# Attention, a gated layer and a mixture of experts on one core: operands of the second layer made at steps of a table, and the last 24 steps of the first layer written by hand

## The chip, the cores and the metric

The kernel runs on one core of a Trainium2 chip. The metric is the device time of one execution in microseconds. TensorE (PE) multiplies, VectorE (DVE), ScalarE (ACT) and GpSimd (POOL) prepare operands and empty the accumulators in PSUM, and the SyncE queue (SP) issues all the transfers. Each engine works through its own instruction list strictly in order; instructions of different engines wait for each other through semaphores.

## The reference

Cut to what is computed:

```python
a   = softmax(p k^T / 8) v                 # 4 batches x 8 heads, 32 packed rows
o   = softmax(q a^T / 8) a                 # 576 rows of each head
x   = o as [2304, 512]
h   = x @ w_in                             # first layer, 512 -> 2048
x   = (h * sigmoid(1.702 h)) @ w_out       # 2048 -> 512
pr  = domain_probs / sum(domain_probs)
out = sum over 4 experts e of pr[:, e] * (relu(x @ w1[e]) @ w2[e])   # second layer, 512 -> 1024 -> 512
```

All inputs are 32 bit floats or wider, and the kernel keeps that precision on TensorE by splitting each operand into a high part (a cast on ACT) and a low part (source minus high part, a subtraction on POOL or DVE), with three matmuls (high·high, low·high, high·low) for each product.

## The kernel before

**First layer.** The tokens are cut into 8 blocks of 288, the hidden width into 4 passes of 512. In a step of a pass `l1_first(a, j, c)` makes hidden chunk c of block j (6 matmuls of 288 columns into one PSUM bank; then two gelu activations on ACT, one giving the high part, and a DVE subtraction on L547 giving the low part), and `l2_first` multiplies the hidden values of the block before with `w_out` (12 matmuls, L556; DVE adds the result to `y` on L581). Step (j, c) below is `l2_first` of block j, chunk of rows c; beside it stands `l1_first` of block j+1. The low part of the last hidden chunk of block j is wanted by the end of step (j, 0).

**Second layer.** 2304 tokens are three pairs of 2 x 384; for each pair 16 quads follow (4 experts x 4 chunks of 256 hidden units), 48 in all, numbered from 0. In a quad, `quad(n)` makes the hidden values by a seven-product scheme (Winograd's form of Strassen's): step k = 0 to 6 holds product k, 6 matmuls of 384 columns on L702, with adds on DVE (L728 to L742), relu on ACT (L710) and the low part on DVE (L711). In steps 1 to 6 `l2_second(n-1, t)` follows, one 128-token tile of the quad before times `w2` (6 matmuls of 512 columns, L765), and DVE adds it, scaled by the probability, to `o` (L776; on ACT, L774, for a pair's first quad). Step 7 has no matmul.

**Operands of the second layer.** The weights of quad n+1 are made during quad n by `w1_operand`: sums s1 to s4 on DVE (L671 to L675), then four casts and subtractions (ACT L156, POOL L157) for S2 and S3; A11 and A12; A22; S1 and S4. Product 0 uses A11, product 1 S2, product 2 S3, product 3 S1, product 4 A12, product 5 A22, product 6 S4. `w2_operand(n)` makes the two halves of `w2` of quad n, which are wanted in quad n+1. The tokens of a pair need four differences T1, T2, T4, T3 (`t_sums`, POOL L618) and for each of seven names a cast of two parts (ACT L636) and two subtractions, one on DVE and one on POOL (L637): `b_operand`, called B0 to B6 below, one for each product. Quads 15 and 31 are the last of a pair (switch quads): during them the next pair's B operands are made, and the T differences in quads 14 and 30.

**What sets the order.** Up to the last 4 steps of the first layer a scheduler of the framework places instructions after its own estimate of times; from there on (L931) each engine gets its instructions in the order in which the code writes them. All operands are generators: each `next` runs one part, at the step where it stands (L949 to L958 for the second layer, `beside` on L922 to L927 for the first pair's). 29 slots of 4.6 KB a partition hold weights, sums and operands; a transfer into a slot waits until the slot's last readers are done. The transfers stand in SP's queue in the order written; during the first quad of a pair the finished rows of the pair before are stored from `l2_second` (L781), and the loads `fetch_w2(n + 1)` at step 5 and `fetch_w1(n + 2)` at the start of the next quad stand behind them.

Of the kernel before, what the change touches and what calls it, by code (L numbers as in the profile page):

```python
# [102 lines left out]
def packed_attention_moe_kernel(  # L103
# [13 lines left out]
    nc = tc.nc  # L117
    B, H, S, D = q.shape
# [11 lines left out]
    CPP = 4  # L130
# [3 lines left out]
    NPAIR = NT // (2 * TB)  # L134
# [14 lines left out]
    def slot(shape, dt, name):  # L149
        return big.tile(shape, dt, tag="b", name=name)  # L150
# [4 lines left out]
    def split(hi, lo, src, eng):  # L155
        nc.scalar.copy(out=hi, in_=src)  # L156
        eng.tensor_sub(out=lo, in0=src, in1=hi.bitcast(F32))  # L157
# [10 lines left out]
    quads = [(i, e, c) for i in range(NPAIR) for e in range(NE) for c in range(w1.shape[2] // 256)]  # L168
    raws = {}
    W = {}  # L170
# [29 lines left out]
    def make_w():  # L200
        order.drain(convert())
# [450 lines left out]
    def w1_operand(n):  # L652


        raw = raws.pop(("w1", n))
        Am = {f"A{m + 1}{k + 1}": raw[:, 2 * k:2 * k + 2, m * 128:(m + 1) * 128] for m in range(2) for k in range(2)}
        S = slot([128, 4, 2, 128], F32, "s")
        s2, s3, s1, s4 = (S[:, x] for x in range(4))

        def operand(names, src):  # L660
            t = slot([128, 2, 2, 2, 128], F32R, "w1")
            hi, lo = t[:, :, 0], t[:, :, 1]
            if len(names) == 1:
                hi, lo = t[:, 0, 0], t[:, 0, 1]
            split(hi, lo, src, nc.gpsimd)
            for o, name in enumerate(names):
                for hl in range(2):
                    for kk in range(2):
                        Wop[n, name, hl, kk] = t[:, o, hl, kk, :]

        nc.vector.tensor_add(out=s1, in0=Am["A21"], in1=Am["A22"])  # L671
        nc.vector.tensor_sub(out=s2, in0=s1, in1=Am["A11"])
        yield
        nc.vector.tensor_sub(out=s3, in0=Am["A11"], in1=Am["A21"])  # L674
        nc.vector.tensor_sub(out=s4, in0=Am["A12"], in1=s2)  # L675
        yield
        operand(("S2", "S3"), S[:, 0:2])
        yield
        yield
        operand(("A11", "A12"), raw[:, :, :128].rearrange("p (o k) f -> p o k f", k=2))  # L680
        yield
        operand(("A22",), Am["A22"])
        yield
        operand(("S1", "S4"), S[:, 2:4])
        yield

    def w2_operand(n):
        raw = raws.pop(("w2", n))
        for c in range(2):
            yield  # L690
            w = W2[n, c] = slot([128, 2, 512], F32R, "w2")
            split(w[:, 0, :], w[:, 1, :], raw[:, c, :], nc.gpsimd)
            yield

    def product(n, k):
        i = quads[n][0]
# [100 lines left out]
    moe = [(packed_w, (0, 0), None)]  # L797
# [22 lines left out]
    pos = {"m": 0}  # L820
# [16 lines left out]
    def moe_step():  # L837
        fn, args, tag = moe[pos["m"]]
        pos["m"] += 1
        part = fn(*args)  # L840
        if part is not None:
            order.drain(part)
        due["n"] = max(due["n"], todo.get(tag, 0))
        if state["cvt"] < due["n"]:
            make_w()
        for part in beside.get(tag, ()):
            next(part, None)
# [10 lines left out]
    def load(what):  # L858
        for t in what.split():
            if t == "F":  # L860
                fetch_w()
            elif (t[0], int(t[1])) not in loaded:
                loaded.add((t[0], int(t[1])))
                (load_kv if t[0] == "k" else load_q)(int(t[1]))
# [4 lines left out]
    def lane(steps):  # L869

        steps = steps.split()
        for i, t in enumerate(steps):
            u = int(t[1])
            need = "kq"[t[0] == "u"] + t[1]
            load(need)
            yield lambda: when[need[0], u]
            part = pack(u) if t[0] == "p" else unpack(u)
            ask = next(part)
            for n in range(1 << 30):
                if n == AHEAD and i + 1 < len(steps):  # L880
                    load("kq"[steps[i + 1][0] == "u"] + steps[i + 1][1])
                t_ = yield ask
                order.at["now"] = t_
                try:
                    ask = part.send(t_)
                except StopIteration:
                    break
            if t[0] == "u":
                finished.append(u)
# [15 lines left out]
    with tc.manual_schedule(engines=engines):  # L905
# [4 lines left out]
        lanes = [lane(x) for x in LANES] + [conversions(2 * CPP, MORE)]  # L910
        for x, back in zip(lanes + [moe_lane()], BACK):
            order.add(x, back)
# [3 lines left out]
    t_parts = {i: t_sums(i) for i in range(NPAIR)}  # L916
    b_parts = {i: b_operand(i) for i in range(NPAIR)}
    last = n_pass1 - 1
    fetch_w1(0)
    fetch_w2(0)  # L920
    first = w1_operand(0)
    beside = {}  # L922
    for c in range(CPP):
        beside["first", last, 3, c] = (t_parts[0],)
        beside["first", last, 4, c] = (first,)
        beside["first", last, 5, c] = (b_parts[0], first)
        beside["first", last, 6, c] = (b_parts[0],)  # L927
    while pos["m"] < len(moe) - CPP:
        moe_step()
    per_pair = len(quads) // NPAIR  # L930
    with tc.manual_schedule(engines=engines):  # L931

        for n in range(len(quads) + 1):
            none = iter(())
            now = quad(n) if n < len(quads) else none
            fetch_w1(n + 1)
            (load_probs, norm_probs)[n]() if n < 2 else None
            after = w1_operand(n + 1) if n + 1 < len(quads) else none
            w2_now = w2_operand(n) if n < len(quads) else none
            tiles = list(range(2 * TB // 128))  # L940
            for k in range(8):
                next(now, None)
                if k > 0:
                    if n == 0:
                        if pos["m"] < len(moe):
                            moe_step()
                    elif tiles:
                        l2_second(n - 1, tiles.pop(0))
                next(after, None)  # L949
                next(w2_now, None)  # L950
                if k == 5:
                    fetch_w2(n + 1)
                after_pair = n // per_pair + 1
                if after_pair < NPAIR:
                    if n % per_pair == per_pair - 2:
                        next(t_parts[after_pair], None)
                    if n % per_pair == per_pair - 1 and k > 0:
                        next(b_parts[after_pair], None)  # L958


# [28 lines left out]
```

## Time and profile before

| | |
|---|---|
| median of 3 runs | 1195.77 us (1195.07 to 1196.13) |
| the profiled execution | 1195.29 us |
| its span, first to last instruction | 1193.5 us |
| mean granted TensorE clock | 0.986 |
| PE busy | 1153.0 us, 97% |
| DVE, ACT, POOL busy | 902.9, 512.0, 465.2 us |

The profile is of one execution. The span lies inside the measured time, 1.8 us short of it. A row of the timeline gives the start in us from the span's start, the length, the engine, the line, the tiles written and read, the shape and how many instructions were merged; in brackets stands how long the engine was idle before, and what it waited for. A row of the waits gives the total, the number of times and the longest one.

### The profile page before, as it was taken

To read this page: it belongs to the slowest core of one execution; us is meant where nothing else is said; L and a number is where in the kernel's file an instruction comes from. 1 tells how busy PE (TensorE), PEld (TensorE's weight loads), DVE (VectorE), ACT (ScalarE), POOL (GpSimd) and SP (SyncE) were. 2 spreads that over 40 slices of the span, in tenths; PEclk is the share of its full clock that TensorE was granted. 3 is DMA by queue.
4 is the path that set the end of the run, shared out by engine and by line. 5 is a ranking of instruction groups with operands and counts; after the bars stand their busy time and mean duration, and the time that the engine had idled before them with its cause. 6 is when DMAs were issued, how large, how long until landed. Compare 5 with 4: busy or idle time off the path is not lost.

```text
span 1193.5 us, 18705 instructions
## 1 busy us (share of the span) xinstructions
PE 1153.0 (97%) x7040; PEld 1045.8 (88%) x7040; DVE 902.9 (76%) x1673; ACT 512.0 (43%) x1144; POOL 465.2 (39%) x385
## 2 busy tenths in 40 slices
PE   6689999999999999999999999999999999999998
PEld 5467899999999898988989878988888788898887
DVE  4976987868766767777778967777779687777775
ACT  4677764444344443333333443333334443333331
POOL 2231211101102434444446754444448554444441
PEclk7799999999999999999999999999999999999999
DMA  9732211211100122222221142222111322211211
GB/s 260 208 118 80 88 54 54 71 53 55 37 18 1 20 71 71 71 71 71 71 70 37 54 141 71 71 71 71 62 45 54 127 86 71 71 57 54 67 54 53
DMA packets 66026, 87.49 MB, mean 73 GB/s; under 512 B 7312, under 2 KB 47248, under 8 KB 65936
## 3 DMA queue, kind: packets, MB, share of 16 engines
q1 hardware_dynamic: 65936, 86.30, 23.9%
q8 instruction: 55, 0.90, 0.3%
q14 instruction: 35, 0.29, 0.1%
HBM read 81.56 MB, written 4.72 MB: 72 GB/s over the span
## 4 chain that ended last, share of the span: by engine, by line
PE 80%; DVE 11%; ACT 3%; DMA 2%; issue 2%; POOL 1%; SPq 0%; DVEq 0%; POOLq 0%; ACTq 0%
PE ps_o L765 29%; PE ps_p L702 25%; PE ps_acc L556 15%; PE ps_h L527 7%; PE ps_w L495 1%; DVE o L776 1%; ACT h L710 1%; DVE h L711 1%; DVE b L637 1%; PE ps_s L311 1%; PE ps_t L298 1%; DVE pw L513 1%; POOL w L157 1%; DMA raw<-in_moe_w_dram 1%; DMA kv<-in_v_dram 1%
## 5 line engine op out<-in xcount | busy, mean ns | idle before, releaser
L765 PE MATMUL ps_o<-w,h 128*128 128x512 f32 x1728 | 445.5, 393 | 0.0
L702 PE MATMUL ps_p<-b,w 128*128 128x384 f32 x2016 | 399.3, 336 | 7.2 <-ACT w L156 3.7
L702 PEld LDWEIGHTS ps_p<-b,w 128*128 128x128 f32 x2016 | 357.9, 188 | 36.8 <-POOL w L157 5.8
L765 PEld LDWEIGHTS ps_o<-w,h 128*128 128x128 f32 x1728 | 320.0, 188 | 50.4
L157 POOL TENSOR_TENSOR w<-raw,w 128x512 fp32r<-128x512 f32 x192 | 229.7, 1196 | 230.7 <-ACT w L156 202.0
L776 DVE SCALAR_TENSOR_TENSOR o<-ps_o,pr,o 128x512 f32<-128x512 f32 x270 | 201.6, 747 | 47.4 <-PE ps_o L765 47.4
L556 PE MATMUL ps_acc<-h,wout 128*128 128x288 f32 x1536 | 230.8, 298 | 4.4 <-DVE h L547 3.7
L556 PEld LDWEIGHTS ps_acc<-h,wout 128*128 128x128 f32 x1536 | 214.4, 190 | 6.9 <-DVE h L547 4.6
L157 POOL TENSOR_TENSOR w<-s,w 128x512 fp32r<-128x512 f32 x96 | 125.2, 1304 | 163.4 <-ACT w L156 163.4
L527 PE MATMUL ps_h<-a,pw 128*128 128x288 f32 x768 | 124.6, 298 | 0.0
L156 ACT CAST w<-s 128x512 fp32r<-128x512 f32 x96 | 58.8, 613 | 126.9 <-DVE s L674 126.9
L527 PEld LDWEIGHTS ps_h<-a,pw 128*128 128x128 f32 x768 | 110.3, 189 | 1.7 <-issue 0.9
L156 ACT CAST w<-raw 128x512 fp32r<-128x512 f32 x192 | 106.6, 555 | 4.9 <-DMA raw<-in_moe_w_dram 4.9
L547 DVE TENSOR_TENSOR h<-g,h 128x288 fp32r<-128x288 f32 x128 | 67.5, 530 | 52.8 <-ACT g L544 52.1
L543 ACT ACTIVATE h<-ps_h 128x288 fp32r<-128x288 f32 x128 | 53.0, 414 | 117.4 <-PE ps_h L527 116.9
L710 ACT ACTIVATE h<-c 128x384 fp32r<-128x384 f32 x48 | 25.2, 525 | 106.7 <-DVE c L736 106.7
L245 POOL TENSOR_TENSOR wout<-cvt,wout 128x512 fp32r<-128x512 f32 x16 | 20.7, 1295 | 114.5 <-ACT wout L243 110.3
L245 POOL TENSOR_TENSOR win<-cvt,win 128x512 fp32r<-128x512 f32 x16 | 21.1, 1321 | 110.7 <-ACT win L243 103.0
L581 DVE TENSOR_TENSOR y<-ps_acc,y 128x288 f32<-128x288 f32 (+2 forms) x120 | 45.0, 391 | 16.5 <-PE ps_acc L556 16.2
L710 ACT ACTIVATE h<-u 128x384 fp32r<-128x384 f32 x48 | 25.2, 525 | 71.5 <-DVE u L742 71.5
L671 DVE TENSOR_TENSOR s<-raw 128x256 f32<-128x256 f32 x48 | 45.2, 942 | 11.9 <-DMA raw<-in_moe_w_dram 6.5
L710 ACT ACTIVATE h<-uv 128x384 fp32r<-128x384 f32 x48 | 25.2, 525 | 67.0 <-DVE uv L742 67.0
(99 smaller groups left out, 1122.8 us busy)
## 6 DMA issues: line engine op xcount, KB each, us to landing
raw<-in_moe_w_dram SPq DMA_DIRECT2D x96, 512.0 KB, 4.0
raw<-in_moe_w_in_dram SPq DMA_DIRECT2D x16, 512.0 KB, 4.5
raw<-in_moe_w_out_dram SPq DMA_DIRECT2D x16, 512.0 KB, 3.7
kv<-in_k_dram SPq DMA_DIRECT2D x16, 288.0 KB, 8.5
q<-in_q_dram SPq DMA_DIRECT2D x32, 144.0 KB, 3.7
out_dram<-o SPq DMA_DIRECT2D x12, 256.0 KB, 2.0
kv<-in_v_dram SPq DMA_DIRECT2D x16, 144.0 KB, 6.8
kv<-in_v_dram SPq DMA_DIRECT2D x8, 288.0 KB, 6.5
```

The lines of the kernel that those rows point to most:

```text
L156: nc.scalar.copy(out=hi, in_=src)
L157: eng.tensor_sub(out=lo, in0=src, in1=hi.bitcast(F32))
L527: nc.tensor.matmul(out=ps[:, :HS], lhsT=PW[a, b, g][:, wp, c * 128:(c + 1) * 128], rhs=A[b * UG + g][:, xp, s * HS:(s + 1) * HS], start=(m ...
L543: nc.scalar.activation(out=h[:, 0, :], in_=ps[:, :HS], func=AF.Gelu_apprx_sigmoid)
L547: nc.vector.tensor_sub(out=h[:, 1, :], in0=g32, in1=h[:, 0, :].bitcast(F32))
L556: nc.tensor.matmul(out=ps[:, :HS], lhsT=W["out", a, c][:, wp, t * 128:(t + 1) * 128], rhs=hid[a, j, c // 2][:, 2 * (c % 2) + hq, :], start ...
L581: nc.vector.tensor_add(out=dst, in0=src, in1=dst)
L671: nc.vector.tensor_add(out=s1, in0=Am["A21"], in1=Am["A22"])
L702: nc.tensor.matmul(out=ps, lhsT=Wop[n, a, wp, kk], rhs=Bop[i, b, xp, kk], start=(m == 0), stop=(m == 5),)
L710: nc.scalar.activation(out=h[:, 0, :], in_=src, func=AF.Relu)
L765: nc.tensor.matmul(out=ps, lhsT=h[:, c, hq, o:o + 128], rhs=W2[n, c][:, wp, :], start=(c == 0 and m == 0), stop=(c == 1 and m == 2),)
L776: nc.vector.scalar_tensor_tensor(out=acc, in0=ps, scalar=pr[:, tok, e:e + 1], in1=acc, op0=ALU.mult, op1=ALU.add,)
```

## The change

`w1_operand` and `w2_operand` return lists of parts instead of being generators, and each part is placed by a table: `W1_AT` and `W2_AT` say at which of a quad's 8 steps it stands, `W1_SWITCH` and `W2_SWITCH` do so for quads 15, 31 and 47. The T differences stand at steps counted back from the pair's first quad (-20 is quad 13, step 4; -17 quad 13, step 7; -13 and -11 quad 14, steps 3 and 5), the B operands at -7, -7, -6, -4, -3 (quad 15, steps 1, 1, 2, 4, 5) and at 1 and 2 of the pair's first quad. For the first pair `FIRST_PAIR` spreads sums (T, W) and operands (W, B) over the steps (3, 0) to (6, 3) of the first layer's last pass. The last 24 steps before the final 4 (the first is `l1_first` of block 5, chunk 0) move under `manual_schedule`, so that from there on every engine has the written order. TensorE's list and SP's are the same in both kernels, instruction for instruction; only DVE, ACT and POOL change.

```diff
--- before.py
+++ after.py
@@ -28,6 +28,14 @@
 UNITS_DONE = 6
 MORE = 4
 AHEAD = 10
+BY_HAND = 24
+W1_AT = (1, 1, 2, 3, 4, 5)
+W1_SWITCH = (1, 1, 2, 4, 5, 4)
+W2_AT = (0, 4)
+W2_SWITCH = (2, 3)
+T_AT = (-20, -17, -13, -11)
+B_AT = (-7, -7, -6, -4, -3, 1, 2)
+FIRST_PAIR = ("", "", "WT", "TT", "TWWB", "WB", "", "", "BW", "BW", "BW", "B", "", "B", "", "B")
 BACK = (0, -0.29, 0.6, 0.7)
 
 
@@ -668,29 +676,31 @@
                     for kk in range(2):
                         Wop[n, name, hl, kk] = t[:, o, hl, kk, :]
 
-        nc.vector.tensor_add(out=s1, in0=Am["A21"], in1=Am["A22"])
-        nc.vector.tensor_sub(out=s2, in0=s1, in1=Am["A11"])
-        yield
-        nc.vector.tensor_sub(out=s3, in0=Am["A11"], in1=Am["A21"])
-        nc.vector.tensor_sub(out=s4, in0=Am["A12"], in1=s2)
-        yield
-        operand(("S2", "S3"), S[:, 0:2])
-        yield
-        yield
-        operand(("A11", "A12"), raw[:, :, :128].rearrange("p (o k) f -> p o k f", k=2))
-        yield
-        operand(("A22",), Am["A22"])
-        yield
-        operand(("S1", "S4"), S[:, 2:4])
-        yield
+        def sums_a():
+            nc.vector.tensor_add(out=s1, in0=Am["A21"], in1=Am["A22"])
+            nc.vector.tensor_sub(out=s2, in0=s1, in1=Am["A11"])
+
+        def sums_b():
+            nc.vector.tensor_sub(out=s3, in0=Am["A11"], in1=Am["A21"])
+            nc.vector.tensor_sub(out=s4, in0=Am["A12"], in1=s2)
+
+        return [
+            sums_a,
+            sums_b,
+            lambda: operand(("S2", "S3"), S[:, 0:2]),
+            lambda: operand(("A11", "A12"), raw[:, :, :128].rearrange("p (o k) f -> p o k f", k=2)),
+            lambda: operand(("A22",), Am["A22"]),
+            lambda: operand(("S1", "S4"), S[:, 2:4]),
+        ]
 
     def w2_operand(n):
         raw = raws.pop(("w2", n))
-        for c in range(2):
-            yield
+
+        def one(c):
             w = W2[n, c] = slot([128, 2, 512], F32R, "w2")
             split(w[:, 0, :], w[:, 1, :], raw[:, c, :], nc.gpsimd)
-            yield
+
+        return [lambda c=c: one(c) for c in range(2)]
 
     def product(n, k):
         i = quads[n][0]
@@ -918,25 +928,28 @@
     last = n_pass1 - 1
     fetch_w1(0)
     fetch_w2(0)
-    first = w1_operand(0)
+    first = (f() for f in w1_operand(0))
     beside = {}
-    for c in range(CPP):
-        beside["first", last, 3, c] = (t_parts[0],)
-        beside["first", last, 4, c] = (first,)
-        beside["first", last, 5, c] = (b_parts[0], first)
-        beside["first", last, 6, c] = (b_parts[0],)
-    while pos["m"] < len(moe) - CPP:
+    for at, what in enumerate(FIRST_PAIR):
+        beside["first", last, 3 + at // CPP, at % CPP] = [{"T": t_parts[0], "B": b_parts[0], "W": first}[x] for x in what]
+    while pos["m"] < len(moe) - CPP - BY_HAND:
         moe_step()
     per_pair = len(quads) // NPAIR
     with tc.manual_schedule(engines=engines):
-
+        while pos["m"] < len(moe) - CPP:
+            moe_step()
+
+        later = []
         for n in range(len(quads) + 1):
             none = iter(())
             now = quad(n) if n < len(quads) else none
             fetch_w1(n + 1)
             (load_probs, norm_probs)[n]() if n < 2 else None
-            after = w1_operand(n + 1) if n + 1 < len(quads) else none
-            w2_now = w2_operand(n) if n < len(quads) else none
+            switch = n % per_pair == per_pair - 1
+            if n + 1 < len(quads):
+                later += [(8 * n + at, f) for at, f in zip(W1_SWITCH if switch else W1_AT, w1_operand(n + 1))]
+            if n < len(quads):
+                later += [(8 * n + at, f) for at, f in zip(W2_SWITCH if switch else W2_AT, w2_operand(n))]
             tiles = list(range(2 * TB // 128))
             for k in range(8):
                 next(now, None)
@@ -946,16 +959,15 @@
                             moe_step()
                     elif tiles:
                         l2_second(n - 1, tiles.pop(0))
-                next(after, None)
-                next(w2_now, None)
+                for at, part in [x for x in later if x[0] == 8 * n + k]:
+                    part()
                 if k == 5:
                     fetch_w2(n + 1)
-                after_pair = n // per_pair + 1
-                if after_pair < NPAIR:
-                    if n % per_pair == per_pair - 2:
-                        next(t_parts[after_pair], None)
-                    if n % per_pair == per_pair - 1 and k > 0:
-                        next(b_parts[after_pair], None)
+                for i in range(1, NPAIR):
+                    when_ = 8 * (n - i * per_pair) + k
+                    for part, slots in ((t_parts[i], T_AT), (b_parts[i], B_AT)):
+                        for x in range(slots.count(when_)):
+                            next(part, None)
 
 
 # ---- launch: one core; inputs and outputs as the reference has them ----
```

In the listings a `w` of 128x2x256 from `raw` is A11 and A12, one of 128x256 from `raw` is A22, one from `s` is S2 and S3 or S1 and S4, one of 128x512 is half a `w2`; line numbers of the changed kernel are 8 to 10 higher.

ACT in the first layer's last pass, before: L543 and the row behind it are a chunk's gelus, and the first row is S2 and S3 of quad 0.

```order
L156 CAST w_4977<-s 128x2x256
L636 CAST b<-y_1062 128x384 x2
L636 CAST b<-T_4838 128x384
L156 CAST w_5038<-raw_2077 128x2x256
L543 ACTIVATE h<-ps_h 128x288
L544 ACTIVATE g_4848<-ps_h 128x288
L636 CAST b<-T_4838 128x384
L156 CAST w_5072<-raw_2077 128x256
L636 CAST b<-T_4893 128x384 x2
L543 ACTIVATE h<-ps_h 128x288
L544 ACTIVATE g_4875<-ps_h 128x288
L156 CAST w_5107<-s 128x2x256
```

The two gelu pairs, of steps (4, 3) and (5, 0) of `l1_first`, stand among ten casts that the scheduler put there. The same engine and place now, from the gelus of `l1_first` of block 5, chunk 0:

```order
L551 ACTIVATE h<-ps_h 128x288
L552 ACTIVATE g_4906<-ps_h 128x288
L164 CAST w_4928<-s 128x2x256
L644 CAST b<-y_1062 128x384 x2
L551 ACTIVATE h<-ps_h 128x288
L552 ACTIVATE g_4944<-ps_h 128x288
L164 CAST w_4962<-raw_2077 128x2x256
L644 CAST b<-T_4892 128x384 x2
L551 ACTIVATE h<-ps_h 128x288
L552 ACTIVATE g_4978<-ps_h 128x288
L551 ACTIVATE h<-ps_h 128x288
L552 ACTIVATE g_5003<-ps_h 128x288
```

The gelu pairs of block 4 are now all ahead of the first cast, and a step has one weight cast and one pair of B casts at most, or none.

POOL in quads 13 and 14 before: T_7359 is T1, T_7383 T2, T_7405 T4 and T_7430 T3, and the first row is S1 and S4 of quad 14.

```order
L157 TENSOR_TENSOR w_7340<-s,w_7340 128x2x256
L618 TENSOR_TENSOR T_7359<-y_1521 128x768
L157 TENSOR_TENSOR w_7380<-raw_7320,w_7380 128x512
L618 TENSOR_TENSOR T_7383<-y_1521,T_7359 128x768
L157 TENSOR_TENSOR w_7402<-s,w_7402 128x2x256
L618 TENSOR_TENSOR T_7405<-y_1521,T_7383 128x768
L157 TENSOR_TENSOR w_7427<-raw_7320,w_7427 128x512
L618 TENSOR_TENSOR T_7430<-y_1521 128x768
L157 TENSOR_TENSOR w_7450<-raw_7343,w_7450 128x2x256
L157 TENSOR_TENSOR w_7471<-raw_7343,w_7471 128x256
L157 TENSOR_TENSOR w_7494<-s,w_7494 128x2x256
```

All four differences stand in quad 14, between its weight subtractions. POOL at the same place now (T_7302 is T1, T_7345 T2, T_7428 T4, T_7477 T3); the first row is half of `w2` of quad 13.

```order
L165 TENSOR_TENSOR w_7299<-raw_7177,w_7299 128x512
L626 TENSOR_TENSOR T_7302<-y_1521 128x768
L165 TENSOR_TENSOR w_7322<-s,w_7322 128x2x256
L626 TENSOR_TENSOR T_7345<-y_1521,T_7302 128x768
L165 TENSOR_TENSOR w_7361<-raw_7325,w_7361 128x512
L165 TENSOR_TENSOR w_7402<-s,w_7402 128x2x256
L165 TENSOR_TENSOR w_7425<-raw_7347,w_7425 128x2x256
L626 TENSOR_TENSOR T_7428<-y_1521,T_7345 128x768
L165 TENSOR_TENSOR w_7448<-raw_7347,w_7448 128x256
L165 TENSOR_TENSOR w_7451<-raw_7325,w_7451 128x512
L165 TENSOR_TENSOR w_7472<-s,w_7472 128x2x256
L626 TENSOR_TENSOR T_7477<-y_1521 128x768
```

T1 and T2 have moved into quad 13, T4 and T3 stand late in quad 14.

ACT from step 4 of quad 15 into quad 16, before: `h<-p` is the relu behind product 4, and the row after it casts A11 and A12 of quad 16.

```order
L710 ACTIVATE h_7499<-p_7508 128x384
L156 CAST w_7612<-raw_7497 128x2x256
L636 CAST b<-T_7359 128x384 x2
L710 ACTIVATE h_7499<-uv 128x384
L156 CAST w_7639<-raw_7497 128x256
L636 CAST b<-y_1521 128x384 x2
L710 ACTIVATE h_7500<-u 128x384
L156 CAST w_7667<-s 128x2x256
L636 CAST b<-T_7405 128x384 x2
L636 CAST b<-y_1521 128x384 x2
L724 COPY p_7692<-ps_p 128x384
L156 CAST w_7717<-raw_7642 128x512
```

Four pairs of B casts follow that of A11 and A12, two of them after the quad's last relu. The same engine from step 3 of quad 15 now, `h<-c` being the relu behind product 3:

```order
L720 ACTIVATE h_7501<-c_7578 128x384
L164 CAST w_7591<-raw_7475 128x512
L720 ACTIVATE h_7500<-p_7509 128x384
L164 CAST w_7612<-raw_7497 128x2x256
L164 CAST w_7615<-s 128x2x256
L644 CAST b<-T_7302 128x384 x2
L720 ACTIVATE h_7500<-uv 128x384
L164 CAST w_7642<-raw_7497 128x256
L644 CAST b<-y_1521 128x384 x2
L720 ACTIVATE h_7501<-u 128x384
L734 COPY p_7682<-ps_p 128x384
L164 CAST w_7684<-raw_7645 128x512
```

The cast of A11 and A12 still stands behind the relu of product 4 in this quad, S1 and S4 directly behind it, and only two B operands are cast between it and the next quad's first copy (`p<-ps`).

## Rows read from the trace of the kernel before

**Rows 1.** Part 1 of the page: busy us, share of the span, instructions
```profile
PE 1153.0 (97%) x7040; PEld 1045.8 (88%) x7040; DVE 902.9 (76%) x1673; ACT 512.0 (43%) x1144; POOL 465.2 (39%) x385
```
**Rows 2.** Waits, 330 us to the end: total us, times, longest
```profile
PE ps_p L702 <- ACT w L156: 3.7, 4, 1.2
PE ps_p L702 <- POOL w L157: 3.5, 6, 0.8
...
PE ps_acc L556 <- DVE h L547: 2.8, 2, 1.5
```
**Rows 3.** Timeline of PE, steps (3, 1), (4, 0) and (4, 3)
```profile
381.83 1.78 PE L556 MATMUL ps_acc<-h,wout 128*128 128x288 f32 x12
...
389.04 1.22 PE L556 MATMUL ps_acc<-h,wout 128*128 128x288 f32 x8
...
401.05 1.23 PE L556 MATMUL ps_acc<-h,wout 128*128 128x288 f32 x8
```
**Rows 4.** Busy time by stretch: us, PE, PEld, DVE, ACT, POOL, clock, DMA
```profile
394.00:398.00 4.00, 4.00 (x21) 4.00 (x21) 4.00 (x6) 2.46 (x7) 4.00 (x4) 0.57 0.00 0
```
**Rows 5.** Timeline of PE: first products of quads 16, 17, 19, 20, 32, 35
```profile
670.12 0.51 PE L702 MATMUL ps_p<-b,w 128*128 128x384 f32 x2
...
688.01 0.61 PE L702 MATMUL ps_p<-b,w 128*128 128x384 f32 x2 [1.10 <-ACT w L156]
...
721.93 2.24 PE L702 MATMUL ps_p<-b,w 128*128 128x384 f32 x12
...
737.57 2.25 PE L702 MATMUL ps_p<-b,w 128*128 128x384 f32 x12
...
925.25 0.51 PE L702 MATMUL ps_p<-b,w 128*128 128x384 f32 x2
...
978.07 2.25 PE L702 MATMUL ps_p<-b,w 128*128 128x384 f32 x12
```
**Rows 6.** Part 5 of the page: busy us, mean ns, idle before
```profile
L547 DVE TENSOR_TENSOR h<-g,h 128x288 fp32r<-128x288 f32 x128 | 67.5, 530 | 52.8 <-ACT g L544 52.1
L543 ACT ACTIVATE h<-ps_h 128x288 fp32r<-128x288 f32 x128 | 53.0, 414 | 117.4 <-PE ps_h L527 116.9
...
L581 DVE TENSOR_TENSOR y<-ps_acc,y 128x288 f32<-128x288 f32 (+2 forms) x120 | 45.0, 391 | 16.5 <-PE ps_acc L556 16.2
```
**Rows 7.** Groups of instructions by line, 400 us to the end
```profile
L637 DVE TENSOR_TENSOR b<-T,b 128x384 fp32r<-128x384 f32 x8 | 8.0, 998 | 0.0
L618 POOL TENSOR_TENSOR T<-y,T 128x768 f32<-128x768 f32 x4 | 7.8, 1952 | 0.0
...
L636 ACT CAST b<-T 128x384 fp32r<-128x384 f32 x16 | 7.4, 510 | 0.0
```
**Rows 8.** Busy time by stretch: quad 13
```profile
623.20:638.84 15.64, 15.64 (x79) 14.06 (x78) 12.02 (x22) 5.54 (x12) 7.33 (x6) 1.00 0.19 66
```
**Rows 9.** Timeline of DVE, quads 13 to 17
```profile
627.88 0.42 DVE L675 TENSOR_TENSOR s<-raw,s 128x256 f32<-128x256 f32 x1
...
644.30 2.07 DVE L675 TENSOR_TENSOR s<-raw,s 128x256 f32<-128x256 f32 x1
...
667.87 0.55 DVE L742 TENSOR_TENSOR p<-ps_p,p 128x384 f32<-128x384 f32 x1
...
675.55 0.75 DVE L776 SCALAR_TENSOR_TENSOR o<-ps_o,pr,o 128x512 f32<-128x512 f32 x1
...
698.69 0.43 DVE L671 TENSOR_TENSOR s<-raw 128x256 f32<-128x256 f32 x1 [5.43 <-POOL w L157]
```
**Rows 10.** Timeline of POOL: A11 and A12 of quads 16 and 18
```profile
669.56 1.29 POOL L157 TENSOR_TENSOR w<-raw,w 128x512 fp32r<-128x512 f32 x1 [0.75 <-ACT w L156]
...
705.18 1.27 POOL L157 TENSOR_TENSOR w<-raw,w 128x512 fp32r<-128x512 f32 x1 [0.32 <-ACT w L156]
```
**Rows 11.** Timeline of SP's queue, quad 17
```profile
693.72 0.39 SPq L644 DMA_DIRECT2D raw<-in_moe_w_dram  x1
```
**Rows 12.** Timeline of DVE, quad 33
```profile
954.85 0.43 DVE L671 TENSOR_TENSOR s<-raw 128x256 f32<-128x256 f32 x1 [6.47 <-DMA raw<-in_moe_w_dram]
```

## The prediction

> **What bounds the kernel now.** I read the page's busy time first: TensorE is busy 97% of the span [rows 1], so time can only come from stretches in which it stands still or runs slowly. TensorE's list is the same in both kernels, so no matmul is saved. Next, the waits: behind 330 us TensorE waits for three things only, the casts (3.7 us) and subtractions (3.5 us) that make the second layer's weights, and the low part of hidden values (2.8 us) [rows 2]. Everything ahead of that is untouched. Then the timeline of TensorE, to price each place with what hangs on the wait:
>
> - First layer's end. Three steps take 389.04 − 381.83 = 7.21 us, 2.40 each; the three from 389.04 to 401.05 take 12.01 [rows 3]. Excess 4.80 us. 2.8 of it is the wait; most of the rest is the clock, granted at 0.57, near the lower of its two levels (1.2 against 2.4 GHz), from 394 to 398 after TensorE had stood [rows 4].
> - First switch. A normal quad takes 737.57 − 721.93 = 15.64 us; quads 16 to 18 take 721.93 − 670.12 = 51.81 instead of 46.92 [rows 5]. Excess 4.89 us.
> - Second switch. Quads 32 to 34 take 978.07 − 925.25 = 52.82 [rows 5]. Excess 5.90 us.
>
> Sum 15.59 us. That is all the change can give; the other quads run at 15.64 without a wait.
>
> **First layer's end, part by part.** Before, a low part (DVE, L547) is late because ACT has ten casts around two gelu pairs and DVE has B subtractions in between. Afterwards block 4's gelus and subtractions stand ahead of all B work, so both stalls at (4, 0) go, and the low clock with them. What is late next: in steps (4, 0) to (5, 3) DVE does 0.53 + 0.39 + 1.00 = 1.92 us (hidden, y, one B) [rows 6, 7], under the 2.40 of a step. ACT's heaviest steps are two gelus, one weight cast (0.7, a B cast's 0.51 scaled to a third more columns) and two B casts: 2 x 0.41 + 0.7 + 2 x 0.51 = 2.5 [rows 6, 7], a little over a step, and two empty steps (4, 2) and (4, 3) follow the first pair. One more wait is new: at (4, 0) the cast of S2 and S3 stands ahead of the next gelus and waits for sums that DVE does after y. I estimate 2 us of lateness there, made up in the empty steps before the low part of chunk 3 is wanted. I leave 0.3 us, bounds 0 and 2.5.
>
> **The switches: why they stall.** DVE has 12.02 us of work in a normal quad of 15.64 [rows 8], 3.6 us spare. While POOL makes a T difference (1.95 us [rows 7]) a DVE sum takes 2.07 us instead of 0.42 [rows 9]: 1.65 lost. Four of them in quad 14 may lose 6.6, 3.0 more than the spare time; then the B subtractions come at 1.0 each. At the end of quad 15 DVE empties the last tile at 675.55 + 0.75 = 676.3, 6.2 us behind TensorE, which began quad 16 at 670.12 [rows 5, 9]. ACT's casts stand behind relus that wait for DVE, so A11 and A12, wanted by the next quad's product 0, come late.
>
> From a quad's first product, S: 42 matmuls of 384 columns and 36 of 512 in 15.64 us make a product 1.04 and a tile 1.39. Product 3 ends at S + 6.9, product 4 at S + 9.4; the low part of A11 is wanted by the third matmul of the next quad, S + 15.99.
>
> **Quad 15 to 16.** The cast keeps its place behind product 4. From DVE's add of that product (667.87) to the low part's end (669.56 + 1.29 = 670.85) are 3.0 us [rows 9, 10], so DVE may lag 3.6. It lagged 4.0: S was 670.12 − 15.64 = 654.48 and the add stood at S + 13.4. Now only T4 and T3 (3.3 us lost at most) stand in quad 14, and the sums of quad 15 move from step 0 to step 1, which lets DVE catch up first. But both sums and B0 and B1 then come in step 1, B2 in step 2: 3 x 1.0 plus 0.5 to 1.5 lost in the sums. Lag 3.5 to 4.5 again, stall 0 to 0.9; I take 0.3.
>
> **Quad 16 to 17.** A11 and A12 move from step 4 to 3: the lag may be 15.99 − 6.9 − 3.0 = 6.1, where step 4 allowed 3.6. Two B subtractions (steps 1 and 2) replace those that ran over from quad 15; I expect a lag of 5 to 5.5, against more than 6. The wait of 1.10 and what follows it [rows 5] go; 0.1 left, bounds 0 and 1.5. B5 and B6 are wanted at products 5 and 6, four steps after they are made: a new wait only with a lag above 5 at step 1.
>
> **Quad 17 to 18.** Here a transfer decides. The sums need `w1` of quad 18, whose load stands behind the last store, and that behind DVE's last add of quad 16. Issued at 693.72, it lets the sums begin at 698.69, 5.0 us later [rows 9, 11], and A11's low part ends at 705.18 + 1.27 = 706.45, 7.8 us after [rows 10]. SP's list is unchanged, so this chain stays. The issue came 693.72 − (688.01 − 1.10) = 6.8 us after quad 16's last tile [rows 5, 11]; with DVE lagging somewhat less I take 6.0, and the last part is one step (2.4) shorter, since A11 moves from step 4 to 3: S + 6.0 + 5.0 + 5.4 = S + 16.4 against 15.99. I leave 0.5 at the first switch and 1.0 at the second, where DVE waited longer, 6.47 us, for this load [rows 12]; bounds 0 and 2.
>
> Normal quads: W2's first half moves from step 1 to 0, and its slot is free, so its load issued, a quad earlier; A11, S1 and S4 move one step earlier; the spare 3.6 us cover the rest. Zero.
>
> **Sum.** Left over: 0.3 + (0.3 + 0.1 + 0.5) + (0.3 + 0.1 + 1.0) = 2.6. Gain 15.6 − 2.6 = 13.0. The profiled execution took 1195.29, so 1182.3; the median shown is 0.48 above that, so 1182.8.
>
> By the Trainium skill (SBUF — State Buffer, Who interferes with whom), a VectorE instruction with two SBUF inputs and a GpSimd instruction that reads SBUF exclude each other for a whole instruction, whichever began first. The trace agrees: 2.07 us beside a T difference of 1.95 [rows 7, 9]. By that rule spreading the differences over two quads takes away no blocked time, only moves it, and the switch part of the gain could fail, which is the first rival.
>
> **Rivals.**
> 1. *DVE's lag stays.* B0, B1 and all sums in step 1 bunch the very instructions that POOL blocks; if DVE is again over 6 us behind, the stalls at the switches stay in half or whole. Against it: half the differences stand in a quad that has 3.6 us spare, and two of three boundaries get a step more. Half left (5.4): 1195.8 − 15.6 + 5.4 + 0.3 = 1185.9; all left (10.8): 1191.3. Chance 0.20.
> 2. *The loads behind the stores bound the third boundary as before*: what follows 688.01 at the first switch, 721.93 − 688.01 − 2 x 15.64 = 2.6 us [rows 5], stays at both, 5.2 in all, because ACT now meets the wait for `w2` at step 0, ahead of everything in quad 17. 1195.8 − 15.6 + 5.2 + 0.9 = 1186.3. Chance 0.11.
> 3. *Slower: the written order of the first layer.* If ACT and DVE need more than 2.40 us in the steps with B work, each of the six heavy steps ends late, ACT's gelus fall behind and TensorE waits in each. A third of a step, 0.8 us, in 6 steps is 4.8, no worse than now; a whole step in each is 14.4, and half clock over those 14.4 us of matmul costs as much again: 1195.8 − 15.6 + 28.8 + 2.3 = 1211. It decides from about 15.6 us of new stall. The budgets 1.92 and 2.5, with two empty steps between, speak against it. Chance 0.04.
> 4. *It does not take effect*: gains and new waits cancel within 0.2% (2.4 us, about what a measurement tells from no change): 1195.8. Chance 0.05.
>
> The forecast keeps 0.60. Faster 0.60 + 0.20 + 0.11 = 0.91, less 0.01 for the edge of rival 1: 0.90; same 0.05; slower 0.05. The forecast's own bounds: nothing left over, 1195.8 − 15.6 = 1180.2; all upper bounds, 2.5 + 2 x 4.4 = 11.3 left, 1191.5, not all together. The range 1179.6 to 1189.0 takes in the forecast, rival 2 and most of rival 1.
>
> **What would show it.** In the new profile: no wait of L556's matmuls for the low part at (4, 0) and the clock at 1.00 there; three quads at each switch in 47 to 48.5 us; TensorE's waits for ACT and POOL at the product line below 2.5 us; DVE at most 5.5 us behind at the end of quads 15 and 16. The third boundary should be the worst left, behind a DMA wait of the sums. A wait of products 5 or 6 in quad 16, a DVE lag of 6 or more, or a stall in steps (4, 1) to (6, 3) would prove a step wrong.

## The result, and the profile after

The changed kernel takes 1180.08 us (median, 1179.69 to 1182.92), the kernel before 1195.95 beside it; the ratio is 0.9872, 95% interval [0.9855, 0.9890], or 15.3 us less [13.2, 17.3]. The forecast was 1182.8. The profiled execution took 1179.71 with a span of 1177.8. One execution each of e1 and e2 (below) took 1406 us at a granted clock of 0.75 and enters no ratio.

Page of the changed kernel, part 1 and three rows of part 5 (busy us, mean ns, idle time before), against [rows 1, 2]:

```profile
PE 1149.0 (98%) x7040; PEld 1044.1 (89%) x7040; DVE 873.1 (74%) x1673; ACT 512.8 (44%) x1144; POOL 461.3 (39%) x385
```
```profile
L775 PE MATMUL ps_o<-w,h 128*128 128x512 f32 x1728 | 445.5, 393 | 0.0
L712 PE MATMUL ps_p<-b,w 128*128 128x384 f32 x2016 | 396.6, 335 | 0.0
...
L564 PE MATMUL ps_acc<-h,wout 128*128 128x288 f32 x1536 | 229.4, 297 | 1.6 <-DVE h L555 0.9
```

TensorE does not wait once in the second layer. DVE is 29.8 us less busy with the same 1673 instructions, which the forecast had not foreseen.

PE's timeline, the steps (3, 1), (4, 0) and (4, 3) of [rows 3] with the hidden chunk made beside (4, 0) (L535), then products of quads 16, 17, 19, 20, 32 and 35 as in [rows 5] (an x12 row holds products 0 and 1):

```profile
381.74 1.78 PE L564 MATMUL ps_acc<-h,wout 128*128 128x288 f32 x12
...
388.94 1.77 PE L564 MATMUL ps_acc<-h,wout 128*128 128x288 f32 x12
390.55 0.96 PE L535 MATMUL ps_h<-a,pw 128*128 128x288 f32 x6
...
396.18 1.77 PE L564 MATMUL ps_acc<-h,wout 128*128 128x288 f32 x12
...
665.25 2.24 PE L712 MATMUL ps_p<-b,w 128*128 128x384 f32 x12
...
680.89 2.24 PE L712 MATMUL ps_p<-b,w 128*128 128x384 f32 x12
...
712.17 2.24 PE L712 MATMUL ps_p<-b,w 128*128 128x384 f32 x12
...
727.81 2.24 PE L712 MATMUL ps_p<-b,w 128*128 128x384 f32 x12
...
915.49 2.25 PE L712 MATMUL ps_p<-b,w 128*128 128x384 f32 x12
...
962.41 2.25 PE L712 MATMUL ps_p<-b,w 128*128 128x384 f32 x12
```

Three steps from (4, 0) on take 7.24 us instead of 12.01, both triples of quads 46.92 instead of 51.81 and 52.82. The clock from 394 to 398 us, 0.57 before [rows 4], is full; the second row is a normal quad (12), where DVE has 11.45 us of work and had 12.02 [rows 8]:

```profile
394.00:398.00 4.00, 4.00 (x32) 4.00 (x31) 4.00 (x5) 2.29 (x7) 3.62 (x3) 1.00 0.10 31
...
602.69:618.33 15.64, 15.64 (x79) 14.06 (x78) 11.45 (x22) 5.55 (x11) 7.27 (x6) 1.00 0.23 69
```

From step (3, 1) to quad 35 TensorE needs 962.41 − 381.74 = 580.67 us; before, 596.24. The difference, 15.57, is the whole gain between the profiled executions (1195.29 − 1179.71 = 15.58). What a kernel takes over 580.67 us on that path is called its stall below. The table splits it by place, both switches added; a boundary's stall is counted up to the end of the next quad's first two products. The runs' ratios are uncertain by 0.2%, 2.4 us, and the profiled executions differ by up to 3 us ahead of (3, 1) (380.6 to 383.6) without an edit there, so small differences are read from the stall. Lag is the time from the end of the last tile that TensorE makes in quad 16 to the end of DVE's add of it; in a normal quad it is 1.0.

| kernel | ratio to before, 95% | first layer | 15 to 16 | 16 to 17 | 17 to 18 | lag |
|---|---|---|---|---|---|---|
| before | 1 | 4.8 | 1.1 | 5.7 | 4.0 | 6.4 |
| changed | 0.9872 [0.9855, 0.9890] | 0 | 0 | 0 | 0 | 2.7 |
| e1_first_alone | 0.9956 [0.9939, 0.9972] | 0 | 1.2 | 7.9 | 1.8 | 6.4 |
| e2_second_alone | 0.9915 [0.9898, 0.9931] | 4.9 | 0 | 0 | 0 | 2.8 |
| e3_old_T | 0.9889 [0.9870, 0.9907] | 0 | 1.3 | 0 | 0 | 4.6 |
| e4_old_B | 0.9865 [0.9846, 0.9884] | 0 | 0 | 0 | 0.3 | 4.3 |
| e5_old_W | 0.9904 [0.9884, 0.9924] | 0 | 0 | 2.0 | 2.8 | 4.9 |
| e6_new_W_only | 0.9896 [0.9874, 0.9918] | 0 | 1.9 | 0 | 2.2 | 5.2 |
| e7_scheduler | 0.9915 [0.9895, 0.9935] | 6.5 | 0 | 0 | 0 | 2.8 |
| e8_old_first_pair | 0.9859 [0.9834, 0.9883] | 0 | 0 | 0 | 0 | 2.7 |
| e9_old_sums | 0.9897 [0.9876, 0.9918] | 0 | 0 | 0 | 1.5 | 5.0 |
| e10_old_casts | 0.9916 [0.9891, 0.9942] | 0 | 0 | 1.4 | 3.6 | 5.3 |
| e11_old_W_spread_T | 0.9924 [0.9905, 0.9944] | 0 | 0 | 2.3 | 3.7 | 5.0 |
| e12_plain | 0.9880 [0.9862, 0.9897] | 0 | 0 | 0 | 0.8 | 4.1 |

### The profile page after: what moved, and what is told of

Same layout as the page of the kernel before. It is cut to its first block, busy times and chain, and to the rows that moved or that the text cites. A ratio compares the mean times of both kernels' runs of the same rounds, so it can differ in the third digit from the quotient of the medians.

```text
span 1177.8 us, 18623 instructions
## 1 busy us (share of the span) xinstructions
PE 1149.0 (98%) x7040; PEld 1044.1 (89%) x7040; DVE 873.1 (74%) x1673; ACT 512.8 (44%) x1144; POOL 461.3 (39%) x385
## 4 chain that ended last, share of the span: by engine, by line
PE 93%; DVE 3%; DMA 3%; ACT 1%; issue 0%; POOL 0%; SPq 0%; DVEq 0%; POOLq 0%; ACTq 0%
PE ps_o L775 34%; PE ps_p L712 30%; PE ps_acc L564 16%; PE ps_h L535 8%; PE ps_w L503 1%; PE ps_s L319 1%; PE ps_t L306 1%; DMA raw<-in_moe_w_out_dram 1%; DMA kv<-in_v_dram 1%; DMA raw<-in_moe_w_in_dram 1%; DVE pw L521 1%; PE ps_v L398 0%; PE ps_e L388 0%; DMA kv<-in_k_dram 0%; DVE t L478 0%
## 5 line engine op out<-in xcount | busy, mean ns | idle before, releaser
L165 POOL TENSOR_TENSOR w<-raw,w 128x256 fp32r<-128x256 f32 (+1 forms) x192 | 227.4, 1194 | 227.2 <-ACT w L164 223.8
L535 PE MATMUL ps_h<-a,pw 128*128 128x288 f32 x768 | 124.4, 297 | 0.0
L535 PEld LDWEIGHTS ps_h<-a,pw 128*128 128x128 f32 x768 | 110.1, 189 | 1.8 <-issue 1.1
L164 ACT CAST w<-raw 128x256 fp32r<-128x256 f32 (+1 forms) x192 | 103.0, 559 | 6.9 <-DMA raw<-in_moe_w_dram 6.9
L738 DVE TENSOR_TENSOR u<-ps_p,p 128x384 f32<-128x384 f32 x48 | 26.6, 555 | 45.4 <-ACT w L164 43.0
L721 DVE SCALAR_TENSOR_TENSOR h<-p,h 128x384 fp32r<-128x384 f32 x48 | 31.4, 654 | 30.8 <-ACT h L720 30.8
```

Of the source, the lines that this page charges most:

```text
L535: nc.tensor.matmul(out=ps[:, :HS], lhsT=PW[a, b, g][:, wp, c * 128:(c + 1) * 128], rhs=A[b * UG + g][:, xp, s * HS:(s + 1) * HS], start=(m ...
```

## Experiments

All diffs are against the changed kernel, most cut to their new lines; W means the weights' parts.

**The two halves.** e1 has only the first layer's part, e2 only the second layer's.

```diff
 e1
-W1_AT = (1, 1, 2, 3, 4, 5)
+W1_AT = (0, 1, 2, 4, 5, 6)
...
+W1_SWITCH = (0, 1, 2, 4, 5, 6)
+W2_AT = (1, 3)
+W2_SWITCH = (1, 3)
+T_AT = (-16, -15, -14, -13)
+B_AT = (-7, -6, -5, -4, -3, -2, -1)
 e2
+BY_HAND = 0
+FIRST_PAIR = ("T", "T", "T", "T", "W", "W", "W", "", "BW", "BW", "BW", "B", "B", "B", "B", "")
```

> Only the first layer's part of the change: its last 24 steps in written order and the new places of sums, weights and B operands there; the second layer has the old places. If the two parts do not touch each other, the 4.8 us of excess in steps (4, 0) to (5, 1) go and the 10.8 us at the two switches stay: 1191.0 us (1190.5 to 1191.6), no wait of TensorE between 330 and 430 us, quads 16 to 18 again 51.8 us and quads 32 to 34 52.8. If the first layer's part also sets how far DVE lags later (rival), the switches change as well and the time is below 1189 or above 1193.

> Only the second layer's part: the new tables for sums, weights, T differences and B operands; the first layer is ordered by the scheduler with the old places. By the theory that the parts add: 1195.8 - 10.8 = 1185.0 us (1184.5 to 1185.6), steps (3, 1) to (5, 1) with the same 4.8 us of excess and the clock near 0.57 from 394 to 398 us, all quads 15.64 us. By the rival that a low clock or a late start in the first layer feeds the switches: over 1187.

e1 keeps 10.84 us of stall, all at the switches, e2 4.93, all in the first layer: together 15.8 against 15.57. The parts add in their sum. The places within e1 do not stay the same: 16 to 17 takes 7.9 instead of 5.7, and 17 to 18 takes 1.8 instead of 4.0. In e1 alone the granted clock falls at 16 to 17, to 0.63 from 684 to 688 us and to its lower level, 0.50, from 940 to 942, after waits of 1.12 and 0.74 us; the kernel before has the same waits there (1.10 and 0.75, 1.12 and 0.73) and a clock of 1.00 at both switches. Why it fell is open.

**Which half of the first layer's part.** e7 gives the last 24 steps back to the scheduler and keeps the new places; e8 keeps the written order and goes back to the old places.

```diff
 e7
+BY_HAND = 0
 e8
+FIRST_PAIR = ("T", "T", "T", "T", "W", "W", "W", "", "BW", "BW", "BW", "B", "B", "B", "B", "")
```

> The changed kernel, but the last 24 steps of the first layer are placed by the scheduler again, with the new table of which sums and operands stand beside which step. If the written order is what counts (forecast): the casts and B subtractions get ahead of gelus and low parts again, a wait of TensorE for the low part at (4, 0) or near it, with a clock under 1.00 behind it: 1183 to 1186 us. If the new places alone do it (rival): 1180.1 and no wait behind 330 us.

> The changed kernel with the last 24 steps of the first layer in written order, but with the old places of the sums and operands: T at (3, 0) to (3, 3), the weights' parts one a step from (4, 0), B operands one a step from (5, 0) to (6, 2). If the written order is what counts: no step has more than two gelus, a weight cast and two B casts, 2.5 us on ACT against 2.40, and DVE 1.92, so no wait behind 330 us and 1180.1 us, within 0.6. If the places count as well (rival): B operands in seven steps running, (5, 0) to (6, 2), push ACT behind by some tenths a step, a wait for the low part in (5, 3) to (6, 3), 1 to 4 us: 1181 to 1184.

PE's timeline and two rows by stretch of e7:

```profile
389.80 1.22 PE L564 MATMUL ps_acc<-h,wout 128*128 128x288 f32 x8
393.38 0.99 PE L564 MATMUL ps_acc<-h,wout 128*128 128x288 f32 x3 [2.36 <-DVE h L555]
395.56 0.61 PE L564 MATMUL ps_acc<-h,wout 128*128 128x288 f32 x1 [1.19 <-DVE h L555]
```
```profile
396.00:400.00 4.00, 4.00 (x18) 4.00 (x18) 4.00 (x5) 1.84 (x5) 4.00 (x4) 0.50 0.18 51
```

Under the scheduler the new places are worse than the old (6.5 us against 4.8): the waits of 2.36 and 1.19 for a low part are back, and behind them the clock is at its lower level (0.50); the 1186.7 us are a little over the range expected. e8 has no stall. The written order is all that this part needs; the new places are not what helps, against the rival in both expectations.

**The switches, one table at a time.** e3, e4 and e5 put T, B and W back, e6 both T and B.

```diff
 e3, e6
+T_AT = (-16, -15, -14, -13)
 e4, e6
+B_AT = (-7, -6, -5, -4, -3, -2, -1)
 e5
+W1_AT = (0, 1, 2, 4, 5, 6)
+W1_SWITCH = (0, 1, 2, 4, 5, 6)
+W2_AT = (1, 3)
+W2_SWITCH = (1, 3)
```

> The changed kernel with the four T differences back in quad 14 (steps 0 to 3) and quad 30; everything else new. By the forecast's theory (DVE's spare time in quad 13 pays for half of what POOL blocks) DVE's lag at the end of quad 14 rises by 2 to 3 us over the changed kernel's 3.3, the cast of A11 and A12 behind product 4 of quad 15 is late again, and 1 to 2 us of stall return at each switch: 1182 to 1184 us. By the rival (the differences only move blocked time, their place is of no matter, and the earlier casts and the two B operands moved on did it all): 1180.1 us within 0.5, and no wait of TensorE behind 330 us.

> The changed kernel with the seven B operands back at one a step in the switch quads, so that none is left for the first quad of a pair. By the theory of the lag: DVE's B subtractions before product 4 of quad 15 are as many as in the changed kernel, so the boundary of quads 15 and 16 stays whole; DVE's lag in quad 16 is 1 to 2 us higher at its start (4 to 5 us instead of 3), still under the 6.1 that the earlier cast of A11 and A12 allows: 1180.1 to 1180.8 us. By the rival (B5 and B6 in quad 16 are what brought the lag down): a lag of 6 or more in quad 16, and the third boundary's 2.6 us come back at both switches: 1185 us.

> The changed kernel with the weights' parts back at their old steps (sums at 0 and 1, S2 and S3 at 2, A11 and A12 at 4, A22 at 5, S1 and S4 at 6, w2 at 1 and 3); T differences, B operands and the first layer stay new. Theory of the lag: in the changed kernel the low part of A11 and A12 of quad 18 ends about 2.9 us before TensorE wants it; a step later takes 2.4 of that away, and the sums that fall beside POOL's subtractions (0.93 us instead of 0.45 for the first) raise the lag by 0.5 a quad: 0 to 1 us of stall at each switch, 1180.1 to 1182. Rival (the earlier casts of A11 and A12 are what the switch part rests on): the waits of quads 16 to 17 and 17 to 18 come back, 1.1 + 2.6 us at each switch, 1187.

> The changed kernel with the four T differences and the seven B operands at their old places; only the weights' parts and the first layer are new. Theory of the lag: it is the old one in quads 14 and 15 less what the sums lose no more (about 0.5 a quad), so near 5 at the end of quad 15 and 5 to 7 in quad 16; stall at the boundary of quads 15 and 16 as before or a bit less (0.5 to 1.3), at that of 17 and 18 half of before (1 to 2), none between: 2 to 3 us at each switch, 1184 to 1186. Rival (weights alone do it): no stall, 1180.1.

e3: TensorE waits in quad 16 as expected, 0.7 us a switch, somewhat less than the 1 to 2 expected. Its DVE ends quad 14 with 5.2 us of lag (654.30 + 0.75 − 649.86) instead of the changed kernel's 3.3, a little under the rise expected, and meets POOL in one of quad 15's sums (1.12). It adds product 4 at 663.05, 13.4 us after the quad began (649.69), as late as before:

```profile
666.23 2.01 PE L712 MATMUL ps_p<-b,w 128*128 128x384 f32 x10 [0.38 <-POOL w L165]
```
```profile
654.30 0.75 DVE L786 SCALAR_TENSOR_TENSOR o<-ps_o,pr,o 128x512 f32<-128x512 f32 x1
...
656.54 1.12 DVE L681 TENSOR_TENSOR s<-s,raw 128x256 f32<-128x256 f32 x1
...
663.05 0.55 DVE L752 TENSOR_TENSOR p<-ps_p,p 128x384 f32<-128x384 f32 x1
```

e4 came as expected: a lag of 4.3, and 0.3 us of stall, at the second switch. e5 missed both ways: 2.4 us a switch, over the 0 to 1 of one theory and under the 3.7 of the other. The spare 2.9 us in that expectation was misread as well; by the rows below it is 1.8. e6 keeps 2.0 us a switch, at the two places expected, though its lag at the end of quad 15 is 6.9, not near 5. With the old T and B, the new W takes 10.84 − 4.06 = 6.8 us away; with the new ones, it is worth 4.8. The new T and B without the new W (e5) take 10.84 − 4.79 = 6.05 away. So neither is enough, W is the larger by a little, and the two overlap.

**What in W.** e9 puts only the sums and `w2` back, e10 only the casts behind them.

```diff
 e9
+W1_AT = (0, 1, 2, 3, 4, 5)
+W1_SWITCH = (0, 1, 2, 4, 5, 4)
+W2_AT = (1, 3)
+W2_SWITCH = (1, 3)
 e10
+W1_AT = (1, 1, 2, 4, 5, 6)
+W1_SWITCH = (1, 1, 2, 4, 5, 6)
```

> Splits the run with the weights' parts at their old steps. Here the sums stand at steps 0 and 1 and w2 at 1 and 3 again (so that the first sum falls beside POOL's subtraction and DVE has 12.02 us in a normal quad instead of 11.45), while the casts of A11 and A12, A22, S1 and S4 keep their new, earlier steps. If the earlier cast is what keeps TensorE from waiting: DVE's lag near 5 at the end of quad 16 as with all old steps, the sums of quad 18 again begin about 10.3 us after quad 16's last tile, and no stall at 16 to 17, 0 to 0.3 at 17 to 18: 1179.7 to 1180.5 us. If what the sums lose beside POOL is what counts (rival): stalls of about 1 us at each of 16 to 17 and 17 to 18, 1184.

> The other half: the sums at step 1 and w2 at 0 and 4 as in the changed kernel (11.45 us of DVE work in a normal quad), but A11 and A12 cast at step 4, A22 at 5, S1 and S4 at 6 in every quad. If the lost time of the sums is what counts: DVE's lag stays near 3 in quad 16, the sums of quad 18 begin 8.2 us after quad 16's last tile, and the low part of A11 and A12 ends 0.5 us before TensorE wants it: no stall, 1179.7 to 1180.5 us. If the earlier cast is what counts (rival): 1 us of stall at each of 16 to 17 and 17 to 18, four in all, 1184. Both kernels near 1180 would mean that either half is enough, since each buys more than the 1 us that is short.

The low parts (L721) in the groups by line from 430 to 1160 us, busy us and mean ns: the changed kernel's (behind products 4 and 5), then e9's and e10's worst:

```profile
L721 DVE SCALAR_TENSOR_TENSOR h<-uv,h 128x384 fp32r<-128x384 f32 x47 | 31.7, 675 | 27.8 <-ACT h L720 27.8
L721 DVE SCALAR_TENSOR_TENSOR h<-p,h 128x384 fp32r<-128x384 f32 x46 | 30.3, 658 | 29.5 <-ACT h L720 29.5
```
```profile
L721 DVE SCALAR_TENSOR_TENSOR h<-p,h 128x384 fp32r<-128x384 f32 x47 | 49.8, 1061 | 28.7 <-ACT h L720 28.7
```
```profile
L721 DVE SCALAR_TENSOR_TENSOR h<-uv,h 128x384 fp32r<-128x384 f32 x47 | 52.0, 1107 | 28.6 <-ACT h L720 28.6
```

With half of the table one of the low parts meets POOL in nearly every quad, and the lag is 5.0 and 5.3, as high as with the whole old one (e5). At nearly the same lag the earlier casts (e9) leave 1.5 us and the later ones (e10, e5) 4.8 to 4.9. So e10's first theory fell, because it took the lag for settled by the sums; e9's stall came out between the two, nearer the first; its median of 1184.1 us is the rival's figure. The profiled execution took 1182.5, 2.8 more than the changed kernel's, and 1.4 of that lie ahead of (3, 1), where it has no edit.

**Lag or cast?** e11 has e5's old W, but each T difference in a quad of its own, so that nothing of T is left by quad 15. e12 has the parts that seemed needed and no more.

```diff
 e11, as e5 and
+T_AT = (-52, -41, -28, -17)
 e12
+T_AT = (-52, -41, -28, -17)
+B_AT = (-7, -6, -5, -4, -3, -2, -1)
+FIRST_PAIR = ("T", "T", "T", "T", "W", "W", "W", "", "BW", "BW", "BW", "B", "B", "B", "B", "")
```

> The weights' parts at their old steps, as in the run that had 4.8 us of stall in four places, but with the four T differences of a pair each in a quad of its own (quads 9, 10, 12 and 13; and 25, 26, 28, 29), where DVE has 2.8 us or more to spare. If DVE's lag decides (forecast's theory): the lag at the end of quad 14 falls from 3.0 to about 1, at the end of quad 16 from 4.95 to 3 to 4, the sums of quad 18 begin 8.5 to 9.5 us after quad 16's last tile, and of the 4.8 us 0 to 2 are left: 1180 to 1182.2 us. If the step of the casts decides by itself (rival): 4.8 us stay, 1184.9.

> What the runs so far say is needed, and nothing more: the first layer's last 24 steps in written order with the old places there, the weights' parts at their new steps, one T difference a quad (quads 9, 10, 12, 13), the B operands at their old places. If written order, earlier casts and a small lag suffice: no wait behind 330 us, lag at the end of quad 16 under 4, 1179.5 to 1180.5 us, the same as the changed kernel. If B5 and B6 or the new places of the first pair are needed after all (rival): 0.3 to 1.5 us of stall, 1180.4 to 1181.6.

DVE's timeline in quad 15 of e11, and POOL's beside it:

```profile
655.93 1.64 DVE L645 TENSOR_TENSOR b<-y,b 128x384 fp32r<-128x384 f32 x1
657.50 1.37 DVE L645 TENSOR_TENSOR b<-T,b 128x384 fp32r<-128x384 f32 x1
```
```profile
655.68 1.48 POOL L165 TENSOR_TENSOR w<-s,w 128x512 fp32r<-128x512 f32 x1
657.12 1.33 POOL L645 TENSOR_TENSOR b<-T,b 128x384 fp32r<-128x384 f32 x1
```

The theory that the lag comes from the T differences alone fell: e11's DVE ends quad 14 with 1.0 us of lag, as in any quad, is 4.0 behind within quad 15's first two tiles, and the kernel stalls 6.0 us. Here the lag is made in the switch quad, by B subtractions and sums that run beside POOL's; T differences in quad 14 come on top of that (e3).

e12 keeps 0.8 us, at the second switch, which is its rival's range; its lag is 4.1. As e8 has no stall with the old places of the first pair, e12 lacks the new places of T or B in the second layer; which of them, no run separates, but e4, with the old B alone, keeps 0.3 us at the same place. No run is clear of the changed kernel on the faster side: the ratios of e4 and e8 are lower by less than their intervals, and e8 has the same stall, 0.

## Why the prediction was right, and where its sizes were not

**The places and the sum of the gain: right.** Three stretches with 15.59 us to give were named; 15.57 came out of them. What was forecast to remain, 2.6 us, is the term that was mis-sized: nothing remained, and the forecast of 1182.8 us is 2.7 over the 1180.1 measured. Of the 2.6 us, 2.3 belong to the switches, where DVE's lag was put too high at every boundary. Of the signs named, all held: three quads in 46.92 us, full clock at (4, 0), a lag of 4.3 and 2.9 us at the end of quads 15 and 16, and the third boundary as the one with the least to spare, behind a DMA wait.

**First layer: right in cause, 0.3 too dear.** The lateness of ACT at (4, 0) is there; e8 and e7 show the written order as the cause. ACT's timeline of the changed kernel:

```profile
391.58 0.62 ACT L164 CAST w<-s 128x512 fp32r<-128x512 f32 x1 [1.72 <-DVE s L684]
392.10 0.92 ACT L644 CAST b<-y 128x384 fp32r<-128x384 f32 x2
392.93 0.40 ACT L551 ACTIVATE h<-ps_h 128x288 fp32r<-128x288 f32 x1
```

The gelus of a chunk whose matmuls ended at 390.55 + 0.96 = 391.51 begin 1.4 us later (estimate: 2), and that is made up before the low part is wanted, as forecast.

**Quad 15 to 16: this step failed.** It charged 3 B subtractions at 1.0 and 0.5 to 1.5 us lost in the sums, and came to a lag of 3.5 to 4.5 at product 4 and 0.3 us of stall, where there is none. DVE in quad 15 of the changed kernel, and POOL beside it:

```profile
655.30 0.42 DVE L685 TENSOR_TENSOR s<-raw,s 128x256 f32<-128x256 f32 x1
655.63 0.55 DVE L645 TENSOR_TENSOR b<-y,b 128x384 fp32r<-128x384 f32 x1
656.10 0.55 DVE L645 TENSOR_TENSOR b<-T,b 128x384 fp32r<-128x384 f32 x1
...
657.70 0.55 DVE L645 TENSOR_TENSOR b<-T,b 128x384 fp32r<-128x384 f32 x1
...
660.44 0.55 DVE L752 TENSOR_TENSOR p<-ps_p,p 128x384 f32<-128x384 f32 x1
...
668.82 0.74 DVE L786 SCALAR_TENSOR_TENSOR o<-ps_o,pr,o 128x512 f32<-128x512 f32 x1
```
```profile
653.29 1.02 POOL L645 TENSOR_TENSOR b<-T,b 128x384 fp32r<-128x384 f32 x1
656.12 1.70 POOL L165 TENSOR_TENSOR w<-s,w 128x512 fp32r<-128x512 f32 x1 [1.81 <-ACT w L164]
657.77 1.63 POOL L165 TENSOR_TENSOR w<-raw,w 128x512 fp32r<-128x512 f32 x1
```

POOL is idle from 654.31 to 656.12; nearly all of the sums and the first two B subtractions begin in that gap, the third just ahead of POOL's next instruction (657.77), and they take 0.42 and 0.55 us. Before, the four sums took 3.2 us here (1.00, 1.40, 0.41, 0.42) and the three B subtractions 2.3 (0.55, 0.59, 1.14), against 1.7 and 1.7 now, and DVE came into the quad with 3.7 us of lag instead of 3.3. Product 4 is added at 660.44, 10.8 us after the quad began (665.25 − 15.64 = 649.61): 1.4 us of lag, where 4.0 stood before and 3.6 are allowed. The 1.0 us from [rows 7] is a mean in which three subtractions of four ran beside POOL; whether they would do so again was not asked of the new order. By the forecast's measure DVE is 668.82 + 0.74 − 665.25 = 4.3 us behind at the quad's end, inside its "at most 5.5".

**Quad 16 to 17: right in its stall**, 0.1 forecast, 0 measured, with a lag about half of the 5 to 5.5 expected. DVE in quad 16 of the changed kernel, the add of product 3:

```profile
674.61 0.55 DVE L746 TENSOR_TENSOR c<-ps_p,uv 128x384 f32<-128x384 f32 x1
```

That is 2.5 us after S + 6.9, where 6.1 are allowed. By the forecast's own limit for the later cast, 3.6, so small a lag would not have needed the earlier one. Still the step's reason, the earlier cast, holds in e3, e4, e6 and e9, which have lags of 4.3 to 5.2, the earlier cast, and no stall there, while the later cast with 4.9 to 5.3 stalls 1.4 to 2.3 us.

**Quad 17 to 18: the chain was right, its start was not.** DVE and SP of the changed kernel, against [rows 9, 11], and POOL's A11 and A12:

```profile
683.05 0.75 DVE L786 SCALAR_TENSOR_TENSOR o<-ps_o,pr,o 128x512 f32<-128x512 f32 x1
683.72 0.55 DVE L738 TENSOR_TENSOR u<-ps_p,p 128x384 f32<-128x384 f32 x1
689.41 0.43 DVE L680 TENSOR_TENSOR s<-raw 128x256 f32<-128x256 f32 x1 [5.15 <-DMA raw<-in_moe_w_dram]
```
```profile
683.82 0.34 SPq L791 DMA_DIRECT2D out_dram<-o  x1
684.26 0.39 SPq L652 DMA_DIRECT2D raw<-in_moe_w_dram  x1
```
```profile
693.82 2.31 POOL L165 TENSOR_TENSOR w<-raw,w 128x512 fp32r<-128x512 f32 x2 [1.09 <-ACT w L164]
```

The last store leaves when DVE has added quad 16's last tile (683.80), the load of `w1` next, 3.4 us into the quad (680.89) where 6.0 was forecast and 6.8 stood before; then 5.15 us of transfer (5.0) and 5.7 to the low part's end (5.4; a `w` of 1.30 from 693.82). S + 14.2 instead of S + 16.4, and wanted at S + 15.99: 1.8 us to spare, 0 stall for the forecast's 0.5 and 1.0. The load behind the stores is the next bound all the same: over the kernels with the earlier cast the sums of quad 18 or 34 begin 7.75 to 9.91 us after the last tile without a stall, and where they begin 10.04 to 11.36 us after it, the stall is 0.3 to 1.4.

**The rivals.** The first (lag stays) fell, but half of the stall does stay, 4.8 to 6.0 us, in e5, e10 and e11, at lags of 4.9 to 5.4; the lag of over 6 that it names comes back at the end of quad 15 in e3 and e6 (6.7 and 6.9), which stall 1.3 and 4.1. The Trainium skill (SBUF — State Buffer, Who interferes with whom), that such VectorE and GpSimd instructions lock each other out, agrees with the rows here (0.55 alone, 1.64 beside POOL; adds with an input in PSUM stay at 0.55). What did not follow from it is that the lost time only moves: it goes where the two engines' instructions no longer meet. The second rival's chain is real and had 1.8 us to spare; the third found nothing of its stalls, and the fourth no cancelling. Normal quads cost nothing, as said.

## What to carry to other kernels

Before charging an instruction with its mean from a profile, see what ran beside it there, and whether the new order still puts that beside it: 1.0 us was 0.55. Tables that place work of two engines that block each other are one choice; half of such a table can be as bad as the old one (4.9 us of stall in e10, 4.8 in e5). Where a scheduler orders the last steps ahead of a change of phase, try the plain written order first; it needed no further tuning here (e8).

## What the runs showed of the hardware

DVE's work in a normal quad depends on order alone: 12.02 us before, 11.45 in the changed kernel, 11.94 and 11.88 in e10 and e9, with the same instructions. The first sum had a mean of 929 ns before and has 455 now:

```profile
L671 DVE TENSOR_TENSOR s<-raw 128x256 f32<-128x256 f32 x46 | 42.7, 929 | 11.9 <-DMA raw<-in_moe_w_dram 6.5 <-POOL w L157 5.4
```
```profile
L680 DVE TENSOR_TENSOR s<-raw 128x256 f32<-128x256 f32 x46 | 20.9, 455 | 10.0 <-DMA raw<-in_moe_w_dram 10.0
```
